# Two products in two PSUM banks: one rounding and one subtraction of 1024 columns in the phase step

## The chip, the cores and the metric

The kernel runs on one core of a Trainium2 chip. A core has five engines with an instruction queue each: TensorE (PE: matrix products; its weight loads are shown apart as PEld), VectorE (DVE), ScalarE (ACT), GpSimd (POOL) and SyncE (SP), which issues transfers. Each works its queue off in order and waits at an instruction until what it depends on has been signalled. Products land in PSUM, which has banks of 512 float32 columns on each of 128 partitions.

The metric is the device time of one execution, in microseconds (us). A profile is one execution of its own, recorded by the hardware profiler.

## What is computed

Two sequence mixers run over the same input x of 2048 positions by 640 channels, and a gate made from x blends them:

```python
x = A_u
g = _sigmoid((x * gate_w).sum(-1, keepdims=True))
a = _A_ref(x, A_log_A_real, A_A_imag, A_C_real, A_C_imag, A_log_dt, A_D_skip)
b = _B_ref(x, B_w_r, B_w_i)
return g * a + (1 - g) * b
```

`_B_ref` is a filter in the two-dimensional frequency domain (rfft2, a product with a complex weight, irfft2). `_A_ref` is a long convolution of every channel with a kernel K, plus a skip term. The change lies in the making of K:

```python
A = -jnp.exp(log_A_real) + 1j * A_imag
C = (C_real + 1j * C_imag) * dt[:, None]
P = jnp.exp((A * dt[:, None])[:, :, None] * pos[None, None, :])
K = 2.0 * jnp.einsum("dn,dnl->dl", C, P).real
```

For each channel d and each of 128 states n this needs exponentials of a real part (a magnitude) and the cosine and sine of an imaginary part (a phase), over 2048 positions, summed over n.

## The kernel before

All Fourier transforms are products with cosine and sine tables on PE. `body` runs in two parts. In the first, two generators are interleaved by `merge`: one runs `phase_a` (the forward transforms of x along the sequence, the gate's sums and the whole of the two-dimensional filter) and then `phase_c` (the first transform of K's first part), the other runs `phase_p` (the parameters) and `phase_b` (K). Each `yield x` adds x to its own stream's clock, and `merge` goes on with the stream whose clock, divided by its total (194.0 and 76.8), stands lowest. In the second part `phase_d` multiplies the spectra and transforms back. The merged program is then put in an order on each engine by a planner at compile time, which may let a ready instruction go ahead of an earlier one of the program; a few places pin an order with `issue_after`.

`phase_b` is where the change lies. It makes K for 40 blocks t of 16 channels, in groups of five (`BT = 5`). A position is split into a coarse and a fine part, so that P over 2048 positions is an outer product of a factor x (64 values for each channel and state) and a factor y (32 values). For a group:

- `mags` (L642) is called for each of the five blocks. A matmul of the parameters with the table `rm` gives the real exponents, three chunks of 512 columns, each in a PSUM bank of the pool `b_ps` (L646 to L648); ACT takes the exponential of each into `e` (L650). `b_ps` holds two banks, which all chunks and the phases below take in turn.
- `phases` (L653) is called for each block. A matmul with the table `rp` gives the phase in turns, two chunks of 512 columns (L659). ACT copies a chunk with a large constant MAGIC added, which rounds it to a whole number (L661); DVE subtracts MAGIC and the unrounded value (L662), which leaves the rest of a turn in `q`. Chunk by chunk, with a `yield 0.22` behind each.
- `trig` (L665): DVE takes the absolute value of q (L672), and ACT four sines of 512 columns (L675 to L678) into sc, sx and cx. sx and cx lie in PSUM, a bank each.
- `prods` (L680) of the block before: DVE makes x from e with sx and cx (L685, L686, L687), POOL makes y from e with sc (L689, L690).
- `kgen` (L692) of an older block: PE sums the outer products over the states in a PSUM bank (L703), ACT copies K out (L711).

The exponential and the sine use different tables of ACT, so the five blocks' exponentials stand together, and `issue_after` keeps them behind the sines of the group before and the sines behind them (L649, L674). The parameters of a group are loaded by POOL's queue (L638) into a buffer of two. PSUM's eight banks are all in use: two of `b_ps`, one for K, two for sx and cx, three for the other stream.

Of the kernel before, what the change touches and what calls it, by code (L numbers as in the profile page):

```python
# [9 lines left out]
F32 = mybir.dt.float32  # L10
F32R = mybir.dt.float32r
I32 = mybir.dt.int32
AF = mybir.ActivationFunctionType
ALU = mybir.AluOpType
PSUM = bass.MemoryType.PSUM
# [10 lines left out]
MAGIC = 12582912.0  # L26
# [158 lines left out]
def body(tc, A, out):  # L185
    nc = tc.nc
    T = Ctx()
    with ExitStack() as top:
# [24 lines left out]
        with ExitStack() as cctx:  # L213
            def left():
                with ExitStack() as ctx:
                    T.bc = ctx.enter_context(tc.tile_pool(name="b_c", reuse_waits="tile", bufs=1))
                    T.rm = T.bc.tile([128, 1536], F32R, name="rm")
                    T.rp = T.bc.tile([128, 1024], F32R, name="rp")
                    yield from phase_p(tc, A, T)
                    yield 0.0  # L220
                    yield from phase_b(tc, A, T, ctx)

            ga, gl = chain(phase_a(tc, A, T), phase_c(tc, A, T, cctx)), left()
            next(gl)
            next(ga)
            next(gl)
            while T.pin is None:
                next(ga)
            merge((194.0, ga), (76.8, gl))
            phase_d(tc, A, T, cctx, out)  # L230
# [380 lines left out]
def phase_b(tc, A, T, ctx):  # L611

    nc = tc.nc
    V, G, S, P = nc.vector, nc.gpsimd, nc.scalar, nc.tensor
# [3 lines left out]
    wk = ctx.enter_context(tc.tile_pool(name="b_x", reuse_waits="tile", bufs=3))  # L618
    w2 = ctx.enter_context(tc.tile_pool(name="b_p", reuse_waits="tile", bufs=2))
    w1 = ctx.enter_context(tc.tile_pool(name="b_k", reuse_waits="tile", bufs=1))  # L620
    ps = ctx.enter_context(tc.tile_pool(name="b_ps", reuse_waits="tile", bufs=2, space=PSUM))
    pk = ctx.enter_context(tc.tile_pool(name="b_pk", reuse_waits="tile", bufs=1, space=PSUM))
    pt = ctx.enter_context(tc.tile_pool(name="b_pt", reuse_waits="tile", bufs=1, space=PSUM))
    rp, rm = T.rp, T.rm
# [5 lines left out]

    es, pars, xy, rs = {}, {}, {}, {}
    st = Ctx()
    st.trig = st.exp = None
    after = lambda ins: tc.issue_after(ins.ins) if ins is not None else nullcontext()

# [6 lines left out]
    def mags(t):  # L642
        e = es[t] = ep.tile([128, 16, 96], F32, tag="e", name="e")
        ef = e.rearrange("p d i -> p (d i)")
        for c in range(0, 1536, 512):
            p = ps.tile([128, 512], F32, tag="ps", name="p_e")  # L646
            with after(T.pin):
                P.matmul(p[:, :], pars[t], rm[:, c:c + 512], start=True, stop=True)  # L648
            with after(st.trig):  # L649
                st.exp = S.activation(ef[:, c:c + 512], p[:, :], AF.Exp)  # L650
            yield 0.2

    def phases(t, r):  # L653
        q = wt.tile([128, 2, 16, 32], F32, tag="w", name="q")
        qf = q.rearrange("p v d i -> p (v d i)")
        r.q = qf
        for c in range(0, 1024, 512):
            p = ps.tile([128, 512], F32, tag="ps", name="p_p")
            P.matmul(p[:, :], pars[t], rp[:, c:c + 512], start=True, stop=True)  # L659

            S.activation(qf[:, c:c + 512], p[:, :], AF.Copy, bias=MAGIC)  # L661
            V.scalar_tensor_tensor(out=qf[:, c:c + 512], in0=qf[:, c:c + 512], scalar=MAGIC, in1=p[:, :], op0=ALU.subtract, op1=ALU.subtract)  # L662
            yield 0.22

    def trig(t, r):  # L665

# [48 lines left out]
    def run():  # L715
        pend = []
        load(0)
        for t in range(40):
            if t % BT == 0:
                if t:  # L720
                    prods(t - 1, rs[t - 1])
                    pend.append(t - 1)
                for x in range(t, t + BT):
                    yield from mags(x)
                    if len(pend) > 1:
                        yield from kgen(pend.pop(0))
                if t + BT < 40:
                    load(t + BT)
            rs[t] = Ctx()
            yield from phases(t, rs[t])  # L730
            trig(t, rs[t])
            if t % BT:
                prods(t - 1, rs[t - 1])
                pend.append(t - 1)
            if len(pend) > 2:
                yield from kgen(pend.pop(0))
        prods(39, rs[39])
        for x in (*pend, 39):
            yield from kgen(x)
# [257 lines left out]
```

## Time and profile before

| | us |
|---|---|
| timed runs | 596.81, 605.38, 610.23 |
| their median | 605.38 |
| profiled execution, its own time | 599.3 |
| span of its instructions | 597.5 |

The mean granted clock of TensorE in the profiled execution was 0.965 of full speed. Blocks 0 to 39 have their phases between 69 and 422 us of the span. `phase_d`'s products follow from about 436 us on.

A line of a group of instructions reads: line of the source, engine, operation, what is written and read, partitions x columns, count, then the busy time in us and the mean length of one in ns, then how long the engine stood idle just before these instructions and which instruction ended that. A line of waits names who waited for whom, the total in us, how often, and the longest. A line of a timeline has the start and the length in us, and a count where neighbours of a kind are merged. A line of windows has the stretch, its length, the busy time of PE, PEld, DVE, ACT and POOL with their number of instructions, the granted clock, the share of the transfer engines' time and GB/s.

### The profile page before, as it was taken

The numbers are of one execution on the slowest core, as the hardware profiler recorded it, in microseconds if no ns is written. First come the engines' busy times: TensorE is split into PE (matmuls) and PEld (weight loads), VectorE is DVE, ScalarE is ACT, GpSimd is POOL, SyncE is SP. The second block draws the span as 40 slices with busy tenths as digits, with TensorE's granted clock in tenths as the row PEclk, the third lists the DMA queues.
The fourth block names the chain that finished last, engine by engine and source line by source line (L and its number), as shares of the span: only waits on it lengthen the run. The fifth ranks groups of instructions, "written<-read, shape, count | busy, mean of one in ns | idle before, by whom it ended". The sixth has DMA issues, their size and how long they took to land.

```text
span 597.5 us, 16647 instructions
## 1 busy us (share of the span) xinstructions
PE 532.8 (89%) x7084; PEld 407.4 (68%) x7084; DVE 475.2 (80%) x748; ACT 364.4 (61%) x659; POOL 250.1 (42%) x246
## 2 busy tenths in 40 slices
PE   8688979989979989988798999899889999999974
PEld 6577657766656666676676676566777988897741
DVE  5971597598899989999979888978487586976954
ACT  4556776476748877899688887699822423232210
POOL 4931153053435325325406325406353347547541
PEclk9899999999979998999998998999998999999978
DMA  8788203236620412143240233004694979989875
GB/s 340 294 279 280 83 14 127 98 135 205 243 89 24 136 52 69 53 142 111 90 121 6 71 98 111 23 28 148 212 392 141 356 280 340 319 281 319 258 236 221
DMA packets 48083, 101.98 MB, mean 171 GB/s; under 512 B 3316, under 2 KB 32776, under 8 KB 46248
## 3 DMA queue, kind: packets, MB, share of 16 engines
q1 hardware_dynamic: 24888, 67.74, 32.6%
q10 hardware_dynamic: 20080, 22.52, 11.7%
q0 software_dynamic: 3040, 10.65, 5.3%
q8 instruction: 56, 0.92, 0.6%
q14 instruction: 19, 0.16, 0.1%
HBM read 60.91 MB, written 39.98 MB: 169 GB/s over the span
## 4 chain that ended last, share of the span: by engine, by line
PE 50%; DVE 23%; DMA 10%; ACT 9%; issue 6%; POOL 1%; SPq 0%; ACTq 0%; DVEq 0%; POOLq 0%
PE p_s L336 8%; PE p_eo L565 8%; PE p_s L349 7%; PE p_i L833 4%; PE p_e L648 4%; PE p_k L703 4%; DVE q L662 3%; DMA s_d<-s 3%; PE p_e L161 3%; PE p_c L912 2%; DVE aq L672 2%; DVE x L687 2%; DMA t3e<-s3e_d 2%; DMA u_d<-ut 2%; PE p_p L659 2%
## 5 line engine op out<-in xcount | busy, mean ns | idle before, releaser
L689 POOL TENSOR_TENSOR y<-e,sc 128x512 f32<-128x512 f32 x40 | 55.4, 1384 | 123.5 <-ACT sc L675 80.4
L349 PE MATMUL p_s<-t,w 128*64 128x160 f32 x1056 | 91.5, 311 | 8.4 <-ACT ut L383 4.6
L349 PEld LDWEIGHTS p_s<-t,w 128*64 128x64 f32 x1056 | 76.7, 138 | 17.8 <-ACT ut L383 5.5
L650 ACT ACTIVATE e<-p_e 128x512 f32<-128x512 f32 x120 | 68.5, 601 | 23.9 <-PE p_e L648 21.4
L565 PE MATMUL p_eo<-td,pmt 107*128 107x321 f32 x204 | 67.3, 454 | 6.3 <-ACT pmt L517 6.2
L703 PE MATMUL p_k<-x,y 128*32 128x64 f32 x2560 | 61.0, 224 | 9.4 <-DVE x L687 3.3
L703 PEld LDWEIGHTS p_k<-x,y 128*32 128x32 f32 x2560 | 44.4, 111 | 35.7 <-issue 24.3
L662 DVE SCALAR_TENSOR_TENSOR q<-q,p_p 128x512 f32<-128x512 f32 x80 | 53.4, 680 | 14.9 <-ACT q L661 13.1
L648 PE MATMUL p_e<-rm,par 128*128 128x512 f32 x120 | 58.5, 516 | 5.2 <-ACT e L650 4.4
L337 ACT COPY t<-p_s 128x512 f32<-128x512 f32 x40 | 24.6, 624 | 62.8 <-PE p_s L336 44.7
L690 POOL TENSOR_TENSOR y<-e,sc 128x512 f32<-128x512 f32 x40 | 53.9, 1347 | 7.8 <-ACT sc L676 7.8
L565 PEld LDWEIGHTS p_eo<-td,pmt 107*128 107x128 f32 x204 | 38.4, 196 | 21.9 <-ACT pmt L517 9.2
L687 DVE TENSOR_TENSOR x<-e,cx 128x1024 f32<-128x1024 f32 x40 | 48.4, 1211 | 1.9 <-ACT cx L678 1.9
L661 ACT ACTIVATE q<-p_p 128x512 f32<-128x512 f32 x80 | 46.7, 592 | 4.5 <-PE p_p L659 3.9
L805 DVE TENSOR_TENSOR ma<-p_s,us 128x640 f32<-128x640 f32 (+1 forms) x36 | 28.2, 784 | 25.5 <-PE p_s L349 14.8
L659 PE MATMUL p_p<-rp,par 128*128 128x512 f32 x80 | 44.0, 554 | 4.3 <-DVE q L662 4.3
L833 PE MATMUL p_i<-t,w 128*64 128x160 f32 x528 | 45.0, 308 | 3.1 <-POOL t L811 2.8
L336 PEld LDWEIGHTS p_s<-c,kt 128*64 128x64 f32 x640 | 39.6, 139 | 11.3 <-issue 6.7
L336 PE MATMUL p_s<-c,kt 128*64 128x128 f32 x640 | 44.2, 277 | 3.0 <-ACT q L661 1.6
L835 ACT COPY s<-p_i 128x640 f32<-128x640 f32 x32 | 21.7, 695 | 38.5 <-PE p_i L833 22.4
L833 PEld LDWEIGHTS p_i<-t,w 128*64 128x64 f32 x528 | 38.8, 141 | 7.9 <-POOL t L811 3.6
L811 POOL TENSOR_TENSOR t<-mb 64x320 f32<-64x320 f32 (+1 forms) x36 | 29.7, 824 | 34.4 <-DVE t L811 34.4
(153 smaller groups left out, 1146.4 us busy)
## 6 DMA issues: line engine op xcount, KB each, us to landing
u_d<-ut SPq DMA_DIRECT2D x32, 320.0 KB, 3.2
us<-u_d ACTq DMA_DIRECT2D x16, 640.0 KB, 5.8
s_d<-s ACTq DMA_DIRECT2D x15, 640.0 KB, 6.9
t<-s_d SPq DMA_DIRECT2D x14, 640.0 KB, 6.0
ww<-in_w_l SPq DMA_DIRECT2D x8, 642.0 KB, 3.8
ue<-u_d SPq DMA_DIRECT2D x8, 640.0 KB, 4.5
k_d<-kt SPq DMA_DIRECT2D x4, 1280.0 KB, 7.8
kt<-k_d SPq DMA_DIRECT2D x8, 640.0 KB, 6.0
```

Of the source, the lines that this page charges most:

```text
L336: nc.tensor.matmul(p[64 * ri:64 * ri + 64, j, :], src(i + j), e1[ri], start=True, stop=True)
L349: ins = nc.tensor.matmul(p[64 * j:64 * j + 64, i, 160 * ri:160 * ri + 160], w2[:, x, 64 * ri:64 * ri + 64], t1[:, x // 2 if x < 32 else K0 ...
L565: P.matmul(p[:, :E], st.pmt[:DC, c, w, j, :], tv[:DC, w, c, :], start=c == 0, stop=c == 2)
L648: P.matmul(p[:, :], pars[t], rm[:, c:c + 512], start=True, stop=True)
L650: st.exp = S.activation(ef[:, c:c + 512], p[:, :], AF.Exp)
L659: P.matmul(p[:, :], pars[t], rp[:, c:c + 512], start=True, stop=True)
L662: V.scalar_tensor_tensor(out=qf[:, c:c + 512], in0=qf[:, c:c + 512], scalar=MAGIC, in1=p[:, :], op0=ALU.subtract, op1=ALU.subtract)
L687: V.tensor_tensor(out=x[:, 0].rearrange("p d (h j) -> p d h j", h=2), in0=e[:, :, 0:64].rearrange("p d (h j) -> p d h j", h=2), in1=cx.uns ...
L689: G.tensor_tensor(out=y[:, 1], in0=e[:, :, 64:96], in1=sc[:, 0], op=ALU.mult)
L690: G.tensor_tensor(out=y[:, 0], in0=e[:, :, 64:96], in1=sc[:, 1], op=ALU.mult)
L703: P.matmul(st.pb[32 * r:32 * r + 32, o, :], y[:, ri, 4 * qq + JR[r], :], x[:, ri, 4 * qq + JR[r], :], start=t % 2 + qq + 1 - ri == 0, stop ...
L833: T.mm = P.matmul(p[x:x + 64, i // 2, 160 * (i % 2):160 * (i % 2) + 160], T.w3[:, k0 + h + i, x:x + 64], t2[:, h + i, :], start=True, stop ...
```

## The change

`b_ps` gets one buffer in place of two, and a tile of two banks, `both`, is made once and kept. A magnitude's chunk takes its banks in turn, by the flag `st.turn`. A phase writes its two products side by side into both banks, one directly behind the other, and is then rounded by one ACT instruction and reduced by one DVE instruction of 1024 columns that run over both banks. The two `yield 0.22` become one `yield 0.44` behind both. The number of PSUM banks, the matmuls, the exponentials, the sines and the products are unchanged; 40 ACT and 40 DVE instructions go.

```diff
-    ps = ctx.enter_context(tc.tile_pool(name="b_ps", reuse_waits="tile", bufs=2, space=PSUM))
+    ps = ctx.enter_context(tc.tile_pool(name="b_ps", reuse_waits="tile", bufs=1, space=PSUM))
...
+    both = ps.tile([128, 2, 512], F32, name="p_b")
+    st.turn = 0
...
         for c in range(0, 1536, 512):
-            p = ps.tile([128, 512], F32, tag="ps", name="p_e")
+            p = both[:, st.turn]
+            st.turn ^= 1
             with after(T.pin):
-                P.matmul(p[:, :], pars[t], rm[:, c:c + 512], start=True, stop=True)
+                P.matmul(p, pars[t], rm[:, c:c + 512], start=True, stop=True)
             with after(st.trig):
-                st.exp = S.activation(ef[:, c:c + 512], p[:, :], AF.Exp)
+                st.exp = S.activation(ef[:, c:c + 512], p, AF.Exp)
             yield 0.2
...
-        for c in range(0, 1024, 512):
-            p = ps.tile([128, 512], F32, tag="ps", name="p_p")
-            P.matmul(p[:, :], pars[t], rp[:, c:c + 512], start=True, stop=True)
-
-            S.activation(qf[:, c:c + 512], p[:, :], AF.Copy, bias=MAGIC)
-            V.scalar_tensor_tensor(out=qf[:, c:c + 512], in0=qf[:, c:c + 512], scalar=MAGIC, in1=p[:, :], op0=ALU.subtract, op1=ALU.subtract)
-            yield 0.22
+        for i in range(2):
+            P.matmul(both[:, i], pars[t], rp[:, 512 * i:512 * i + 512], start=True, stop=True)
+
+        p = both.rearrange("p i x -> p (i x)")
+        S.activation(qf, p, AF.Copy, bias=MAGIC)
+        V.scalar_tensor_tensor(out=qf, in0=qf, scalar=MAGIC, in1=p, op0=ALU.subtract, op1=ALU.subtract)
+        yield 0.44
```

## The prediction

> **What bounds the kernel now.** I read the page's totals first, then its groups, for what the touched lines cost:
>
> ```profile
> span 597.5 us, 16647 instructions
> ...
> PE 532.8 (89%) x7084; PEld 407.4 (68%) x7084; DVE 475.2 (80%) x748; ACT 364.4 (61%) x659; POOL 250.1 (42%) x246
> ```
>
> ```profile
> L662 DVE SCALAR_TENSOR_TENSOR q<-q,p_p 128x512 f32<-128x512 f32 x80 | 53.4, 680 | 14.9 <-ACT q L661 13.1
> L687 DVE TENSOR_TENSOR x<-e,cx 128x1024 f32<-128x1024 f32 x40 | 48.4, 1211 | 1.9 <-ACT cx L678 1.9
> ```
>
> ```profile
> L661 ACT ACTIVATE q<-p_p 128x512 f32<-128x512 f32 x80 | 46.7, 592 | 4.5 <-PE p_p L659 3.9
> ...
> L835 ACT COPY s<-p_i 128x640 f32<-128x640 f32 x32 | 21.7, 695 | 38.5 <-PE p_i L833 22.4 <-DMA s_d<-s 10.9 <-DVE mb L806 3.7
> ```
>
> PE leads over the whole span, but the change touches one part of it: products 40 times over (t = 0 to 39, five to a group), between 60 and 435 us. I cut that part by the view of windows into eight phase stretches (five phases each, 69:96 to 399:426) and the seven magnitude stretches between them; the rows are the totals of all, of the phases, and of the magnitudes:
>
> ```profile
> 60.00:435.00 375.00, 338.55 (x4630) 249.53 (x4628) 320.35 (x498) 289.76 (x531) 142.62 (x129) 0.97 0.31 101
> ...
> sum 251.00, PE 217.04 PEld 160.22 DVE 228.79 ACT 197.48 POOL 126.53; mean PE 27.13 PEld 20.03 DVE 28.60 ACT 24.68 POOL 15.82
> ...
> sum 106.00, PE 104.02 PEld 75.83 DVE 86.97 ACT 80.71 POOL 15.34; mean PE 14.86 PEld 10.83 DVE 12.42 ACT 11.53 POOL 2.19
> ```
>
> So magnitudes are PE's (104 of 106 us) and the phases are DVE's (229 of 251 us, 91%, with 22 us idle). Of that idle time the group of L662 owns 14.9 us: the subtraction waits for the rounding. The waits say the same, and show the return path, where ACT waits for a subtraction before its sines and PE waits for a bank:
>
> ```profile
> ACT sc L675 <- DVE q L662: 13.7, 14, 2.3
> DVE q L662 <- ACT q L661: 13.1, 13, 3.0
> ...
> PEld p_p L659 <- DVE q L662: 5.4, 7, 2.2
> ...
> PE p_p L659 <- DVE q L662: 4.3, 4, 2.1
> ```
>
> How two halves overlap today is seen in the timeline. Around 217 us they stay together; first DVE, then PE's weight loads, then ACT, then DVE again some periods later, each row with its start and its length:
>
> ```profile
> 217.33 1.36 DVE L662 SCALAR_TENSOR_TENSOR q<-q,p_p 128x512 f32<-128x512 f32 x2 [0.26 <-ACT q L661]
> ```
>
> ```profile
> 218.07 0.19 PEld L659 LDWEIGHTS p_p<-rp,par 128*128 128x128 f32 x1 [0.16 <-DVE q L662]
> 218.26 0.37 PEld L514 LDWEIGHTS p_t<-c,fg 128*128 128x128 f32 x2
> 218.75 0.19 PEld L659 LDWEIGHTS p_p<-rp,par 128*128 128x128 f32 x1
> ```
>
> ```profile
> 221.57 1.06 ACT L661 ACTIVATE q<-p_p 128x512 f32<-128x512 f32 x2
> 222.52 1.07 ACT L519 COPY ft<-p_t 128x512 f32<-128x512 f32 x2
> ```
>
> ```profile
> 228.79 1.27 DVE L662 SCALAR_TENSOR_TENSOR q<-q,p_p 128x512 f32<-128x512 f32 x2
> 229.99 0.67 DVE L685 SCALAR_TENSOR_TENSOR x<-e,sx 128x512 f32<-128x512 f32 x1
> ...
> 231.79 1.21 DVE L687 TENSOR_TENSOR x<-e,cx 128x1024 f32<-128x1024 f32 x1
> 232.92 1.40 DVE L483 TENSOR_TENSOR fo<-ue 128x640 f32<-128x640 f32 x1
> ```
>
> Around 121 us the planner put other work between the halves, on ACT the sines of the phase before, on DVE a copy and a product:
>
> ```profile
> 120.50 0.63 ACT L675 ACTIVATE sc<-q 128x512 f32<-128x512 f32 x1 [2.30 <-DVE q L662]
> 121.03 0.58 ACT L661 ACTIVATE q<-p_p 128x512 f32<-128x512 f32 x1
> 121.70 0.72 ACT L676 ACTIVATE sc<-aq,c 128x512 f32<-128x512 f32 x1
> ```
>
> ```profile
> 122.18 0.68 DVE L662 SCALAR_TENSOR_TENSOR q<-q,p_p 128x512 f32<-128x512 f32 x1
> 122.78 0.68 DVE L383 COPY t<-p_s 128x512 f32<-128x512 f32 x1
> 123.38 1.21 DVE L687 TENSOR_TENSOR x<-e,cx 128x1024 f32<-128x1024 f32 x1
> 124.51 0.68 DVE L662 SCALAR_TENSOR_TENSOR q<-q,p_p 128x512 f32<-128x512 f32 x1
> ```
>
> **The change part by part.**
>
> *The subtraction (DVE, where the phases are bound).* A duration is not what an instruction costs in a row of them, because the next one starts before it has ended. Two halves start at 228.79 and the next instruction at 229.99: 1.20 us. The 1024 columns of L687 start at 231.79 and the next follows at 232.92: 1.13 us. The wide form with a PSUM operand is not in the trace. Its bounds are 1.13 us (as L687) and 1.36 us (two means of 0.68, no overlap at all), so one phase changes by between -0.07 and +0.16 us. I take 1.13, since the halves of L662 and L687 both follow the column count. Times 40 it is -2.8 us, at worst +6.4. All of it lies on the engine that sets the phases' pace.
>
> The Trainium skill, "Perfetto Trace Analysis", section "Optimizing Scalar/DVE Operations", gives a per-instruction overhead of about 125 ns for DVE and 51 ns for ACT on PSUM, and says that grouping helps a saturated engine. By that the estimate would be 40 x 0.125 = 5.0 us on DVE and 2.0 us on ACT; the 0.07 us of the rows is smaller, though its wide instruction reads SBUF.
>
> *The rounding (ACT).* Two halves take from 221.57 to 222.52, 0.95 us. For 1024 columns I use the slope between L661 and L835, (695 - 592) / 128 = 0.80 ns a column: 592 + 512 x 0.80 = 1004 ns long, with the same overlap (592 - 475 = 117 ns) 0.89 us apart. That is -0.06 x 40 = -2.4 us of ACT; bounds are 0.89 and 1.18 us (two means of 592). ACT is busy 197 of 251 us there, so the saving itself I cost at nothing: DVE's work covers it. Without that cover it is worth the 2.4.
>
> *The hand-over from rounding to subtraction.* This is what the merge gives up. Today the first subtraction runs beside the second rounding. From the second product's end on, the old chain is half a rounding and half a subtraction (0.59 + 0.68 = 1.27 us), the new one a whole of each (1.00 + 1.21 = 2.21), 0.94 us more. Against it, the two products now follow each other directly, and the second is ready earlier wherever work lay between. Where DVE has other work queued (27 of 40 phases at the least, as 13 waits are seen) nothing of it shows. Where it waited, the bounds are 0 and 0.94 us: 13 x 0.94 = 12 us. I take 0.2 each, +2.6 us, near the lower end: in the period at 120 us the subtractions stand 2.33 us apart with DVE occupied, so the first half was early for nothing.
>
> *The bank (PE).* The two subtractions at 217.33 end at about 218.01 (one length of 0.68) and 218.69; PE loads for the next phase's products at 218.07 and 218.75, 0.06 us behind each, with transposes of the other stream between. Now both banks are held until the whole subtraction is through, some 0.6 us later for the first product. PE is in order: queued behind that wait are the other stream's matmuls, for which ACT and DVE wait. The waits of today are 5.4 + 4.3 = 9.7 us in 11. Bounds: 0 (the second product's wait disappears, as it has the same release) and 40 x 0.6 = 24 us. I take 11 x 0.15, +1.6 us, since PE has 34 us idle in the phases and DVE paces them.
>
> *Magnitudes, the turn, yields.* Two banks still alternate, with the same 120 products and exponentials. Fifteen chunks are odd, so every second group ends on bank 0, and the next phase's first product waits for the last exponential: 4 x 0.6 = 2.4 us at most, one exponential each; I take +0.6, as the second product would have waited for it anyway. Both yields become one of the same sum, so the other stream's share is unchanged; its work comes behind both products. No DMA is added or moved; the parameter load on POOL's queue waits for a group's last product, and the pair ends no later than that did, so I cost it at 0, with the two-deep parameter buffer as its cover; without it, 0.6 us for each of the seven later groups, 4 us, would fall on that queue and on the products y behind it.
>
> **Sum.** -2.8 + 0 + 2.6 + 1.6 + 0.6 = +2.0 us, about 601 us for the profiled execution, whose own time was 599.3 us for a span of 597.5. The three timed runs go from 596.81 to 610.23 with a median of 605.38; the mean of the four times is 602.9. On that the forecast is 605 us: no change that can be told, since about 2% (12 us) is what a measurement of this kernel tells from none. Its own range, with the scatter of the runs about their mean (-6 to +7), is 597 to 613.
>
> **The rivals.**
>
> *Slower, by PE's order.* PE stands at the first product until the whole subtraction is done, the other stream's matmuls come late, and DVE, which has no slack, then waits for them. The place is L659, the price 0.3 to 0.6 us in each of 40 phases: +12 to +24 us, about 621 us. It decides once more than half of the phases lose their 0.6. For it: the 0.06 us at 218.07. Against it: the 34 us that PE has idle there, and a planner that can lay other matmuls ahead of the wait. The Trainium skill, "Perfetto Trace Analysis", speaks for it in two places: "Matmuls" has independent groups rotate through banks so that evacuation overlaps the next matmuls, and "Optimizing Scalar/DVE Operations" advises breaking instructions up where an unsaturated engine leaves bubbles on others. No run yet shows either at work here.
>
> *Faster, by an unbroken run of sines.* At 121.03 a rounding stands among the sines; in the new order a whole rounding can only start after both products, behind the sines, so cx ends some 0.5 us earlier. At 0.25 to 0.5 us in each of 40 phases, with the 2.8, that is -13 to -23 us, about 585. It decides once half of DVE's 22 idle us in the phases go this way. Against it: 14.9 of them are waits for the rounding itself, which now ends later.
>
> *The two banks are tracked as one tile.* Then a magnitude's product waits for the exponential of the other bank. The exponentials stand at 108.76 and 110.50, two in 1.74 us:
>
> ```profile
> 108.76 1.08 ACT L650 ACTIVATE e<-p_e 128x512 f32<-128x512 f32 x2 [6.00 <-PE p_e L648]
> 110.50 1.08 ACT L650 ACTIVATE e<-p_e 128x512 f32<-128x512 f32 x2 [0.66 <-PE p_e L648]
> ```
>
> ```profile
> L659 PE MATMUL p_p<-rp,par 128*128 128x512 f32 x80 | 44.0, 554 | 4.3 <-DVE q L662 4.3
> ```
>
> A serial chunk takes a product (0.55, as L659's), an exponential (0.59, as L661's) and two hand-overs (0.06 each, as at 218.07): 1.26 us in place of 0.87, 120 x 0.39 = +47 us, about 650. Nothing in the trace shows one tile's banks apart, but the diff relies on them.
>
> **How the numbers follow.** Forecast 0.60; PE's order 0.21, of which 0.16 beyond 2%; sines 0.16, of which 0.11 beyond 2%; one tile 0.03, all beyond. Faster 0.11, same 0.60 + 0.05 + 0.05 = 0.70, slower 0.16 + 0.03 = 0.19. The range is 595 to 618: it leaves out some 0.08 below and 0.12 above.
>
> **What would show it.** Right: 40 subtractions about 1.13 us apart from their followers, 40 roundings of about 1.0 us, phase stretches within 3% of 251 us in all, DVE's wait for the rounding at 13 to 20 us. Wrong: L659's wait for the subtraction above 20 us (PE's order), DVE idle under 12 us in the phases (sines), or L648 waiting for L650 in nearly each of 120 (one tile).

## The result

The changed kernel is slower. Over six runs of each, taken together, the median is 630.56 us against 603.25 us before; the ratio is 1.047, with a 95% interval of 1.042 to 1.051, so some 28 us. That is outside the range of 595 to 618 us. Medians, here and below, are over all executions of a kernel, while ratios leave out those that fell into a slower state, so a ratio can differ a little from the quotient of two medians.

The page's totals of the changed kernel, and the groups that answer to those of before (L652 and L654 are the magnitudes' product and exponential, L665 and L666 the rounding and the subtraction):

```profile
span 629.2 us, 16597 instructions
...
PE 549.9 (87%) x7084; PEld 412.9 (66%) x7084; DVE 473.1 (75%) x708; ACT 363.9 (58%) x619; POOL 248.1 (39%) x246
...
L654 ACT ACTIVATE e<-p_b 128x512 f32<-128x512 f32 x120 | 71.9, 599 | 54.3 <-PE p_b L652 53.5
...
L666 DVE SCALAR_TENSOR_TENSOR q<-q,p_b 128x1024 f32<-128x1024 f32 x40 | 48.6, 1216 | 8.7 <-ACT q L665 8.7
...
L665 ACT ACTIVATE q<-p_b 128x1024 f32<-128x1024 f32 x40 | 40.7, 1016 | 8.4 <-PE p_b L662 8.0
```

No engine was given more work: PE has the same 7084 matmuls (busy for 17 us longer), and DVE and ACT are a little less busy than before. The two merged instructions have nearly the lengths that the prediction gave them (1216 and 1016 ns). What grew is a wait: ACT stands 53.5 us before exponentials until their product arrives. In the kernel before it was 21.4 us:

```profile
L650 ACT ACTIVATE e<-p_e 128x512 f32<-128x512 f32 x120 | 68.5, 601 | 23.9 <-PE p_e L648 21.4
```

The windows, cut as before into phase stretches (77:102 to 435:465) and the magnitude stretches between them, show where the time is. The first row is the whole part, then the totals of phases and magnitudes:

```profile
60.00:466.00 406.00, 356.14 (x4568) 254.40 (x4568) 318.09 (x459) 290.23 (x491) 140.32 (x129) 0.95 0.30 97
...
sum 231.00, PE 194.53 PEld 141.67 DVE 203.77 ACT 186.15 POOL 114.72; mean PE 24.32 PEld 17.71 DVE 25.47 ACT 23.27 POOL 14.34
...
sum 157.00, PE 144.29 PEld 101.32 DVE 107.20 ACT 94.99 POOL 23.34; mean PE 20.61 PEld 14.47 DVE 15.31 ACT 13.57 POOL 3.33
```

The magnitudes went from 106 to 157 us, the phases from 251 to 231: +51 and -20, together +31, against a span that grew by 31.7. (Outside of these stretches the phases begin 8 us later, at 77 in place of 69 us, and what follows them is 7 us shorter.) Before, PE was busy for 104 of the 106 us of the magnitudes. Now it is idle for 12.7 of 157 while DVE and ACT have 50 and 62 us to spare: no engine fills that stretch, which points to a chain. Part of the other stream's work that stood in the phases is now done in the longer magnitudes, which is why the phases are shorter.

The chain is seen in the timeline. First ACT, then PE, around 275 us of the changed kernel:

```profile
274.48 0.60 ACT L654 ACTIVATE e<-p_b 128x512 f32<-128x512 f32 x1 [0.84 <-PE p_b L652]
274.98 0.58 ACT L519 COPY ft<-p_t 128x512 f32<-128x512 f32 x1
275.67 0.60 ACT L654 ACTIVATE e<-p_b 128x512 f32<-128x512 f32 x1
```

```profile
275.13 0.50 PE L652 MATMUL p_b<-rm,par 128*128 128x512 f32 x1
275.47 0.82 PE L514 MATMUL p_t<-c,fg 128*128 128x128 f32 x6
276.32 0.50 PE L652 MATMUL p_b<-rm,par 128*128 128x512 f32 x1
```

An exponential ends at 275.08, the next product starts at 275.13 and ends at 275.63, its exponential starts at 275.67 and ends at 276.27, and the product after that starts at 276.32. The two products are in different banks, and yet the second waits until the first bank has been read: 1.19 us for this chunk, product, exponential and two hand-overs of 0.04 and 0.05 us. This is a tight one; within a group of five blocks one exponential starts 1.47 us after the other on average, against 1.00 us before. Over the whole trace not one of 119 products starts before the exponential of the chunk before has ended (the least distance is +0.05 us). In the kernel before, 88 of 119 did, and two products could stand back to back:

```profile
249.03 0.87 PE L648 MATMUL p_e<-rm,par 128*128 128x512 f32 x2
```

That is the third rival of the prediction: the two banks are one tile, and accesses to it are put in line as a whole. Two banks of PSUM serve the magnitudes in both kernels; what differs is that the program names them as one tile. It had been given a chance of 0.03. The runs below test it against the second explanation at hand, that PE is held up by a phase keeping both banks.

### The profile page after: what moved, and what is told of

The parts are those of the page before. It is cut to its first block, busy times and chain, and to the rows that moved or that the text cites. A ratio compares the mean times of both kernels' runs of the same rounds, so it can differ in the third digit from the quotient of the medians.

```text
span 629.2 us, 16597 instructions
## 1 busy us (share of the span) xinstructions
PE 549.9 (87%) x7084; PEld 412.9 (66%) x7084; DVE 473.1 (75%) x708; ACT 363.9 (58%) x619; POOL 248.1 (39%) x246
## 5 line engine op out<-in xcount | busy, mean ns | idle before, releaser
L349 PE MATMUL p_s<-t,w 128*64 128x160 f32 x1056 | 95.0, 318 | 9.6 <-ACT ut L383 5.3
L654 ACT ACTIVATE e<-p_b 128x512 f32<-128x512 f32 x120 | 71.9, 599 | 54.3 <-PE p_b L652 53.5
L693 POOL TENSOR_TENSOR y<-e,sc 128x512 f32<-128x512 f32 x40 | 52.7, 1318 | 113.9 <-ACT sc L679 63.9
L707 PE MATMUL p_k<-x,y 128*32 128x64 f32 x2560 | 65.8, 232 | 19.2 <-POOL y L693 6.4
L707 PEld LDWEIGHTS p_k<-x,y 128*32 128x32 f32 x2560 | 47.1, 115 | 52.4 <-issue 31.4
L652 PE MATMUL p_b<-rm,par 128*128 128x512 f32 x120 | 64.6, 538 | 8.8 <-ACT e L654 7.6
L666 DVE SCALAR_TENSOR_TENSOR q<-q,p_b 128x1024 f32<-128x1024 f32 x40 | 48.6, 1216 | 8.7 <-ACT q L665 8.7
L694 POOL TENSOR_TENSOR y<-e,sc 128x512 f32<-128x512 f32 x40 | 52.8, 1320 | 3.7 <-ACT sc L680 3.7
L691 DVE TENSOR_TENSOR x<-e,cx 128x1024 f32<-128x1024 f32 x40 | 48.6, 1216 | 3.7 <-ACT cx L682 3.7
L336 PE MATMUL p_s<-c,u 128*64 128x128 f32 x640 | 45.1, 283 | 2.8 <-ACT ut L383 2.6
L665 ACT ACTIVATE q<-p_b 128x1024 f32<-128x1024 f32 x40 | 40.7, 1016 | 8.4 <-PE p_b L662 8.0
L336 PEld LDWEIGHTS p_s<-c,u 128*64 128x64 f32 x640 | 37.1, 140 | 10.9 <-issue 7.0
```

The source lines that it names most:

```text
L336: nc.tensor.matmul(p[64 * ri:64 * ri + 64, j, :], src(i + j), e1[ri], start=True, stop=True)
L349: ins = nc.tensor.matmul(p[64 * j:64 * j + 64, i, 160 * ri:160 * ri + 160], w2[:, x, 64 * ri:64 * ri + 64], t1[:, x // 2 if x < 32 else K0 ...
L652: P.matmul(p, pars[t], rm[:, c:c + 512], start=True, stop=True)
L654: st.exp = S.activation(ef[:, c:c + 512], p, AF.Exp)
L665: S.activation(qf, p, AF.Copy, bias=MAGIC)
L666: V.scalar_tensor_tensor(out=qf, in0=qf, scalar=MAGIC, in1=p, op0=ALU.subtract, op1=ALU.subtract)
```

## Experiments

**Apart again: magnitudes on two tiles, phases merged.** PSUM has no bank left, so the two-bank pool is closed and opened anew between magnitudes and phases. The magnitudes get two one-bank tiles in it, the phases one two-bank tile.

```diff
-            p = both[:, st.turn]
-            st.turn ^= 1
+            p = st.ps.tile([128, 512], F32, tag="ps", name="p_e")[:, :]
...
+                held.close()
+                held.enter_context(bank("b_m%d" % t, 2))
                 for x in range(t, t + BT):
                     yield from mags(x)
...
+                held.close()
+                held.enter_context(bank("b_f%d" % t, 1))
+                st.both = st.ps.tile([128, 2, 512], F32, name="p_b")
```

> Theory T1 (one tile): the loss comes from the magnitudes, whose products wait for the exponential of the other bank since both banks are one tile. Here the magnitudes have two one-bank tiles again and the phases keep the merged rounding and subtraction, so T1 expects the time of the kernel before, ratio 0.98 to 1.015, and products that start before the previous exponential has ended in at least 60 of 120. Theory T2 (PE's order): holding both banks through the whole subtraction is what costs, so the time stays at that of the changed kernel, ratio 1.03 to 1.055.

Measured: 596.84 us against 601.98 of the kernel before on the same chip, ratio 0.9905 (0.9874 to 0.9936); 89 of 119 products start early. The whole loss is gone with the merged phases still in place, and the time is now 1% below that of the kernel before. That is clear of the interval, but smaller than the 2% that the prediction took as what a measurement can tell. PE's order as the cause falls. The waits of this kernel (L654 and L656 the magnitudes, L664, L667 and L668 the phases):

```profile
ACT e L656 <- PE p_e L654: 21.0, 32, 6.0
...
PEld p_b L664 <- DVE q L668: 9.0, 14, 1.8
...
PE p_b L664 <- DVE q L668: 6.0, 9, 1.7
...
DVE q L668 <- ACT q L667: 3.5, 7, 1.2
```

ACT's wait for products is back at 21 us. PE does wait longer for the merged subtraction (15.0 us; 9.7 before), and it costs nothing that can be seen.

**The other half alone: magnitudes on one tile, phases in halves on two tiles.** Built the same way.

```diff
-            p = ps.tile([128, 512], F32, tag="ps", name="p_e")
+            p = st.both[:, st.turn]
+            st.turn ^= 1
```

> T1: the reverse half of the change alone. Phases in two halves as before, magnitudes in turn on the two banks of one tile: ratio 1.03 to 1.06, with PE's products of the magnitudes behind the exponential before in all of 120. T2: the phases overlap as before, so 0.99 to 1.01.

Measured: 625.98 us, 1.037 (1.029 to 1.044), with 0 of 119 products early. The one tile alone brings most of the 4.7%, without any change to the phases; beside the changed kernel on one chip, further below, it brings all of it.

**Control: the kernel before with the pool closed and opened anew.**

> Control for the way the two experiments are built: the kernel before, with the two-bank pool closed and opened anew between magnitudes and phases. Both theories: 0.985 to 1.015. If it is outside of this, the two experiments are read against this kernel and not against the one before.

Measured: 604.98 us, 1.007 (1.002 to 1.011). The way of building costs 0.7%, far less than the 3.7% of the second experiment, and the first one is below the kernel before in spite of it. So both readings stand.

**No turn at all.** The changed kernel with every magnitude in bank 0.

```diff
-            st.turn ^= 1
```

> The changed kernel with all magnitudes in bank 0, without the turn. T1: the second bank gave nothing, so the time is that of the changed kernel, ratio 1.04 to 1.055. T2 (the two banks do overlap in the magnitudes and the loss is in the phases): the magnitudes become serial on top of it, 120 times some 0.39 us or 47 us more, ratio 1.10 to 1.13.

Measured: 626.25 us, 1.039 (1.034 to 1.045), a hair under the bound of 1.04 that was set and far from 1.10. Alternating between the banks of one tile is worth nothing: using a single bank is as fast. The granted clock is no part of this: it averaged 0.962 over these executions and over those of the kernel before on the same chip.

**Fewer round trips on the one tile.** The changed kernel with two products side by side, one exponential of 1024 columns, then one product and one of 512.

```diff
-        for c in range(0, 1536, 512):
-            p = both[:, st.turn]
-            st.turn ^= 1
-            with after(T.pin):
-                P.matmul(p, pars[t], rm[:, c:c + 512], start=True, stop=True)
+        for c, n in ((0, 2), (1024, 1)):
+            for i in range(n):
+                with after(T.pin):
+                    P.matmul(both[:, i], pars[t], rm[:, c + 512 * i:c + 512 * i + 512], start=True, stop=True)
             with after(st.trig):
-                st.exp = S.activation(ef[:, c:c + 512], p, AF.Exp)
-            yield 0.2
+                st.exp = S.activation(ef[:, c:c + 512 * n], both[:, 0:n].rearrange("p i x -> p (i x)"), AF.Exp)
+            yield 0.2 * n
```

> The changed kernel with fewer hand-overs in the magnitudes: two products side by side, one exponential of 1024 columns over both banks, then one product and one of 512. With one tile (T1) a block has two product-to-exponential round trips in place of three, 2 x 0.93 + 1.0 + 0.6 + some 0.24 against 3 x 1.26, so about 0.5 us less in each of 40 blocks: 20 us less at most, ratio 1.015 to 1.04. If the round trips were not the cost, it stays at 1.04 to 1.05.

Measured: 615.64 us, 1.027 (1.021 to 1.033). Two round trips in place of three take back between a third and a half of the loss, as the ratios stand (1.047 and, in the later run, 1.040 for the changed kernel). The wait of ACT's exponential (here L652) falls with them:

```profile
ACT e L652 <- PE p_b L650: 37.1, 45, 2.8
```

**Where the 1% gain of the first experiment comes from.** Two kernels with its program in half-width instructions; first on the same two-bank tile:

```diff
-        S.activation(qf, p, AF.Copy, bias=MAGIC)
-        V.scalar_tensor_tensor(out=qf, in0=qf, scalar=MAGIC, in1=p, op0=ALU.subtract, op1=ALU.subtract)
+        hv = [(qf[:, 512 * i:512 * i + 512], st.both[:, i]) for i in range(2)]
+        for o, p in hv:
+            S.activation(o, p, AF.Copy, bias=MAGIC)
+        for o, p in hv:
+            V.scalar_tensor_tensor(out=o, in0=o, scalar=MAGIC, in1=p, op0=ALU.subtract, op1=ALU.subtract)
```

> Where does the gain of the first experiment (0.990) come from? Its program, but with two roundings and two subtractions of 512 columns over the two-bank tile, behind both products. Theory W (width): fewer, wider instructions save 2.8 us of DVE and 2.4 us of ACT, so this gives them back: ratio 0.997 to 1.01. Theory O (order): the gain is that both products stand together and the planner lays no other work between the halves, so this keeps it: 0.985 to 0.995.

Measured: 614.14 us, 1.023 (1.019 to 1.027), worse than either theory allowed. In its trace the first subtraction never starts before the second rounding has ended (0 of 40; the least distance is +0.03 us), although they read different banks; in the kernel before 33 of 40 did. That agrees with accesses to the tile being put in line, readers among each other too, but program order alone would allow an early start, so it is the tile or the planner's order that keeps them apart; which of the two is not shown.

Then with each half in a one-bank tile of its own, both products ahead of the halves:

```diff
+        for i in range(2):
+            p = st.ps.tile([128, 512], F32, tag="ps", name="p_p")
+            P.matmul(p[:, :], pars[t], rp[:, 512 * i:512 * i + 512], start=True, stop=True)
+            hv.append((qf[:, 512 * i:512 * i + 512], p))
+        for o, p in hv:
+            S.activation(o, p[:, :], AF.Copy, bias=MAGIC)
+            V.scalar_tensor_tensor(out=o, in0=o, scalar=MAGIC, in1=p[:, :], op0=ALU.subtract, op1=ALU.subtract)
+        yield 0.44
```

> Halves as in the kernel before, each in a one-bank tile of its own, but both products first, then the halves, and one yield of 0.44. W: as the control with reopened pools, 1.0 to 1.012. O: 0.985 to 0.997.

Measured: 604.69 us, 1.007 (1.003 to 1.011), the same as the control. Products side by side and one yield are not what gains; the wide instructions are what is left. From 1.007 to 0.9905 is 1.6%, and the first experiment and the control on its chip are 8 us apart.

Not all of that need be engine time. The granted clock, averaged over the executions that the ratios use, was 0.961 in the first experiment, 0.950 in the control and 0.953 here, against 0.962 and 0.966 of the kernel before on the same two chips. Over 59 such executions of the kernel before, a clock lower by 0.01 goes with some 3.8 us more. By that estimate about 4 of the 8 us go with the clock, and the rest is near the 2.8 us that the rows give for the subtraction. Why these kernels were granted different clocks no run shows.

**One of the two wide at a time.** The first experiment with only the subtraction, and with only the rounding, in halves.

```diff
-        V.scalar_tensor_tensor(out=qf, in0=qf, scalar=MAGIC, in1=p, op0=ALU.subtract, op1=ALU.subtract)
+        for o, p in hv:
+            V.scalar_tensor_tensor(out=o, in0=o, scalar=MAGIC, in1=p, op0=ALU.subtract, op1=ALU.subtract)
```

> One rounding of 1024 columns, two subtractions of 512, one two-bank tile, again, for an interval. By engine time alone (40 x 0.07 us of DVE) 0.99 to 1.0. If the loss of the kernel with both in halves (1.023) comes from the subtraction's side: 1.01 to 1.025.

Measured: 600.33 us, 0.994 (0.989 to 0.999). An earlier run of the same kernel, of four executions from 595.46 to 607.01 us, has a median of 605.35 us against 600.73 and no ratio.

```diff
-        S.activation(qf, p, AF.Copy, bias=MAGIC)
+        for o, p1 in hv:
+            S.activation(o, p1, AF.Copy, bias=MAGIC)
```

> The first experiment with two roundings of 512 columns ahead of its one subtraction. By engine time alone (40 x 0.06 us of ACT, which is not the bound) 0.985 to 1.0. If the 1.023 comes from the rounding's side, since the planner lays sines between the two roundings and the subtraction waits for both: 1.01 to 1.025.

Measured: 600.73 us, 0.9985 (0.994 to 1.003). Against 0.9905, halves in the subtraction alone give back 0.4% and halves in the rounding alone 0.8%, each known to about half a per cent; the engine time of the rows (2.8 and 2.4 us) would be 0.5 and 0.4%. The 3% that both together lose (1.023, in halves on one two-bank tile) is not the sum. The granted clock of that kernel was 0.944, against 0.966 before on that chip, which by the estimate above goes with 8 of its 14 us; the cause of the lower clock and of the rest stays open. The planner lays out another order for each of these kernels.

**Changed kernel and one-tile magnitudes side by side.** The second experiment beside the changed kernel on one chip, to see whether merged phases gain under serial magnitudes too.

> The changed kernel on the chip of the next three, to compare like with like: 1.035 to 1.05.

> Phases in halves on two tiles, magnitudes on one tile, again, beside the changed kernel. If the merged phases gain their 1 to 1.5% with serial magnitudes too, this lies above the changed kernel by that much, 1.045 to 1.065; if the serial magnitudes take the gain, the two lie within 1% of each other, 1.03 to 1.05.

Measured: 628.71 us, 1.040 (1.031 to 1.049), and 622.62 us, 1.038 (1.031 to 1.044). The two cannot be told apart: the gain of the phases is not seen while the magnitudes are serial.

## Why the prediction was wrong

The forecast was no change; the loss came from a mechanism that it named and all but left out. The step that failed is this one, under the magnitudes: "Two banks still alternate, with the same 120 products and exponentials", which was put at nothing (the +0.6 us beside it was for the odd number of chunks). They alternate in address only: 0 of 119 products start before the exponential of the other bank has ended, where 88 did, and the magnitude stretches take 51 us more. The 0.03 for one tile had no row behind it either way; the prediction itself said that nothing in the trace showed one tile's banks apart, and then followed the diff.

Its price was nearer. A serial chunk was put at 1.26 us in place of 0.87, so 0.39 us more. The tightest take 1.18 us, but the mean is 1.47 us, against 1.00 before: 0.47 us more. The magnitude stretches grew by 51 us where +47 was put. The whole grew by only 28, as PE does the other stream's work inside the round trips (40 us more busy in the magnitude stretches), which takes 20 us off the phases; the price of this rival left that out.

The other steps, read where the magnitudes are on two tiles:

- The subtraction and the rounding: lengths of 1.22 and 1.02 us for the 1.21 and 1.00 worked out. The mechanism holds: 33 of 40 subtractions start 1.13 to 1.14 us before the next instruction, where two halves took 1.20, and 30 of 40 roundings 0.90 to 0.92 us before it, where two halves took 0.95. The Trainium skill, "Perfetto Trace Analysis", section "Optimizing Scalar/DVE Operations", by whose overheads per instruction (about 125 ns for DVE and 51 ns for ACT on PSUM) the prediction estimated 7 us in all, points the same way. The trace nearly agrees for ACT, with 0.03 to 0.05 us saved, and shows less for DVE, 0.06 to 0.07 us. Two readings behind this step were wrong without harm: L687 reads not SBUF alone but cx in PSUM too, and a wide form over two banks was in the trace, as L805 multiplies 640 columns from two banks of p_s in 822 ns.
- The hand-over from rounding to subtraction: wrong in its sign. It was to add 2.6 us, and DVE's wait for the rounding to reach 13 to 20 us. It fell from 13.1 to 3.5. A whole rounding is longer than a half, but DVE stood idle for it in only 7 of 40 phases; in the others it had other work.
- The bank: PE's wait for the subtraction rose from 9.7 to 15.0 us, +5 us of waiting where +1.6 us of time was assumed, and the kernel is not slower for it. The slower rival that was given 0.21 is not what happened; in the changed kernel that wait is 10.3 + 7.3 us, under the 20 that would have spoken for it:

```profile
PEld p_b L662 <- DVE q L666: 10.3, 14, 1.9
...
PE p_b L662 <- DVE q L666: 7.3, 9, 1.8
```

- The sum for the phases was +2.0 us; merged phases on two-tile magnitudes measure -5 us against the kernel before, and about -8 against the control, with the clock's part in it. That is within what the forecast called no change, on the other side. The phase stretches of that kernel are 248 us in all, as forecast (within 3% of 251). DVE is idle for 24 us of them. Under 12 us would have spoken for the faster rival by the sines, so that one is not seen either.
- Of the test for one tile, "L648 waiting for L650 in nearly each of 120", the profile shows 71 waits with idle time. The others start no earlier; PE filled the time with other matmuls. The start of each product against the end of the exponential before is the sharper test.

## What to carry to other kernels

Two buffers are two only if whatever orders the accesses sees two objects: before a ring of tiles becomes slices of one larger tile, ask of every use of it, also those that the change is not for, whether its overlap rested on the tiles being apart. This is shown for a tile over two banks of PSUM and not for every tile: the halves of q are one tile in SBUF, and yet in 33 of 40 phases of the kernel before the subtraction of the first half starts before the rounding that writes the second half has ended. Where an alternation matters, look in the trace for a writer that starts before the reader of the other buffer has ended; if none is found, the chance that they are serial is not small, whatever the addresses say. A wide instruction over two banks may be worth having here, but in a pool of its own, opened where it is used; that version, the first experiment, measures 1% below the kernel before.

## What was not expected of the hardware

The wide forms over two PSUM banks behave as the rows of before had it: 1016 ns for the rounding (1004 worked out) and 1216 ns for the subtraction (1211 for L687). At its tightest, as at 275 us, a hand-over between PE and ACT through a PSUM bank takes 0.04 to 0.05 us from the end of the one to the start of the other in the profile's rows, so that nearly all of a serial round trip of 1.19 us is the product and the exponential themselves.
